# Turning the centred rows of the first and last batch on TensorE, with later weight loads and paired score tiles

## The chip, the core and the metric

The kernel runs on one core of one Trainium2 chip, as one launch. The metric is the device time of that launch in microseconds (us), the median of several executions. A profile of one execution says what each engine did: PE is TensorE's matmuls and PEld its weight loads, DVE is VectorE, ACT ScalarE, POOL GpSimd, and SP the queue from which most transfers are issued.

## The reference

Two layers follow each other. The first is a block-sparse causal attention over 4 batches, 8 heads, 768 positions of 64 numbers: each query sees its own block of 64 keys and the three blocks (of 12) whose mean key scores highest.

```python
k_rep = k.reshape(B, H, n_blocks, block, D).mean(axis=3)
gate_scores = np.einsum('bhsd,bhnd->bhsn', q, k_rep)       # causal blocks only
top_idx = np.argsort(gate_scores, axis=-1)[..., -top_k:]   # plus the query's own block
scores = np.where(mask & causal, scale * q @ k.T, -1e9)
out = softmax(scores) @ v
```

The second takes the heads side by side as rows x of 512 numbers, mixes them by a Fourier transform over positions and columns, and puts them through two matrices:

```python
u = x + np.real(np.fft.fft(np.fft.fft(x, axis=1), axis=2))
un = (u - mean(u)) / np.sqrt(var(u) + 1e-06)
out = u + np.maximum(un @ w_ch1, 0.0) @ w_ch2      # w_ch1 512 x 2048, w_ch2 2048 x 512
```

## The kernel before, in words

**Pairs and slots.** Two heads make a pair; 4 pairs make a batch, 16 pairs in all. `attn_slot(i, g, a)` holds the attention work of one slot: the six score tiles of pair i (`stage_S(i, 0..5)`), the gate of pair i+1 (`stage_G`), the turning of q and k of pair i+2 (`stage_A`: twelve 128x128 transposes on TensorE into two PSUM tiles, a reduction `kr` and a copy `q32` on DVE, a cast of the keys on ACT, a copy of the queries on POOL), and the product with v of pair i-1 (`stage_V`, one half for each head, after which DVE divides into the rows x and `stage_fold` adds and subtracts them for the Fourier step). The loads of later pairs are issued on SP at the places where the slot frees their buffers: v of pair i+1 after `cast_v(i-1)`, k and q of pair a+3 after `stage_A(a)`.

**Two kinds of scores.** For the first seven pairs (`P < NX`, NX = 7) a score matmul contracts over 64 rows, the two heads standing in the two halves of the array, and more 64-row matmuls add the mask. From pair 7 on the mask stands in 32 further rows (96 rows, one head at a time), and the gate is `stage_G2` with `stage_K`.

**A batch's second layer.** `stream(b)` is a list of steps: `stage_fg` (DVE), `stage_Y` twice and `stage_M` three times (Fourier steps on TensorE; M's result is added to x on DVE as u, and ACT writes the centred rows, u minus its mean, over x in f16), the turning of these rows into `unT` (six transposing DMAs on SP, in `stage_M`), `stage_R` (variance on DVE, inverse root on POOL), sixteen `stage_W1` (unT with w1, then a relu on ACT or DVE) and `stage_W2` for six row tiles, the last four of which (`held`) are kept for the next batch's stream. In the stream of batch b, `hold_loads` stops the issuing of input loads from before `stage_fg` until `free_loads` after `stage_M`, so that the transposing DMAs meet an empty SP queue; before batch 0 it is called already ahead of slot 4.

**What sets the order.** Slots 1 to 4 run alone; then, for each batch, `weave` merges four slots with one stream: each step has a weight, and the list goes on with whichever of the two has used the smaller share of its own total. A step of weight w that does nothing holds the other steps of its list back by that share. The prologue's order is the written order on every engine. After it the written order binds the SP queue alone; on the other engines a planner, which takes the written order as priority and estimates when operands and buffers are free, sets an order at build time, and each engine then runs its own list strictly in order. All PSUM tiles come from one pool of 4 buffers of two banks each, so a matmul that starts a new tile may have to wait for the engine that reads an old one.

**The constants and weights.** `consts_first` loads the identity and pair 0 and builds `indz` (two 128x768 tiles for the mask) on POOL. The tables `FS` and `FD` for the Fourier steps are loaded on SP ahead of slot 1's loads. w1 comes in four POOL loads (1 MB read each, cast to f16), each behind a one-element POOL copy (`gate`) that reads the weights `pt` of a pair and so sets the earliest time: in the order `load_w1(0,0)`, slot 1, `load_w1(1,1)`, slot 2, `load_w1(2,2)`, slot 3, `load_w1(3,3)`, slot 4.

Of the kernel before, what the change touches and what calls it, by code (L numbers as in the profile page):

```python
# [11 lines left out]
FP = mybir.dt.float32  # L12
# [7 lines left out]
S = 768  # L20
DM = 512
NB = 12
# [106 lines left out]
def kernel(  # L129
# [33 lines left out]
    def ctile(shape, dtype, name):  # L163
        return cpool.tile(shape, dtype, tag=f"c_{name}", name=name)
# [8 lines left out]
    fs_sb = ctile([128, 2, 2, 3, KE], F16, "fs_sb")  # L173
    fd_sb = ctile([128, 6, 256], F16, "fd_sb")
    id32 = ctile([128, 128], FP, "id32")
    oth = ctile([128, 10, NB], F16, "oth")
    czl = ctile([128, 32], F16, "czl")
    czr = ctile([128, S - Q0], F16, "czr")
# [273 lines left out]
    def stage_M(b, kp):  # L452
        u_b, x_b = bpool.tile([128, 2, DM], FP, tag="u_b", name=f"u{kp}_{b}", bufs=5), x_t[b]
        u_t[b, kp] = u_b
        mps = pst([128, 2, 512], f"mx{kp}_{b}")
        for k2 in range(2):
            kt = 2 * kp + k2
            sg = 0 if kt < 3 else 1
            rows = slice(128 * (kt % 3), 128 * (kt % 3 + 1))
            for par in range(2):  # L460
                src = ys[b, par][sg]
                o = mps[:, k2, 256 * par:256 * par + 256]
                nc.tensor.matmul(o, src[:, 0, rows], fd_sb[:, 3 * par, :], start=True, stop=False)
                nc.tensor.matmul(o, src[:, 1, rows], fd_sb[:, 3 * par + 1 + sg, :], start=False,
                                 stop=True)
        if kp == 0:
            un_t[b] = bpool.tile([128, NDT, S], F16, tag="unT", name=f"unT_{b}", bufs=1)
            st_t[b] = [bpool.tile([128, *sh], FP, tag=n, name=f"{n}_{b}", bufs=2)
                       for n, sh in (("mv", [NST, 2]), ("rs", [NST]), ("sm", [NST]))]
        sm = st_t[b][2]  # L470
        for k2 in range(2):
            kt = 2 * kp + k2
            nc.vector.scalar_tensor_tensor(  # L473
                out=u_b[:, k2, :].rearrange("p (m two) -> p two m", two=2),
                in0=mps[:, k2, :].rearrange("p (two m) -> p two m", two=2), scalar=1.0,
                in1=x_b[:, kt, :].rearrange("p (m two) -> p two m", two=2),
                op0=ALU.mult, op1=ALU.add, accum_out=sm[:, kt:kt + 1])
        nm = spool.tile([128, 2], FP, tag="nm", name=f"nm{kp}_{b}")
        nc.vector.tensor_scalar(out=nm, in0=sm[:, 2 * kp:2 * kp + 2],  # L479
                                scalar1=-0.0625 / DM, scalar2=None, op0=ALU.mult)  # L480
        for k2 in range(2):
            nc.scalar.activation(out=x_b[:, 2 * kp + k2, :], in_=u_b[:, k2, :],  # L482
                                 func=AF.Identity, scale=0.0625, bias=nm[:, k2:k2 + 1])
        for kt in range(2 * kp, 2 * kp + 2):
            nc.sync.dma_start_transpose(un_t[b][:, :, 128 * kt:128 * kt + 128], x_b[:, kt, :])

# [60 lines left out]
        nc.gpsimd.tensor_copy(out=dst, in_=src)  # L547

    def consts_first():
        nc.scalar.dma_start(id32, dr["ident32"].ap())  # L550
        load(0, 1, nc.sync)
        load(0, 0, nc.scalar)
        nc.vector.memset(dummy, 1.0)
        nc.scalar.activation(out=dummy, in_=dummy, func=AF.Exp)
        nc.vector.memset(wsrc, 0.0)
        wps = pst([128, 512], "warmps")
        for _ in range(16):
            nc.tensor.matmul(wps, wsrc[:, 0:128], wsrc, start=True, stop=True)  # L558
        nc.vector.tensor_copy(out=dummy, in_=wps[:, 0:1])
        nc.gpsimd.memset(czl, 0.0)  # L560
        nc.gpsimd.memset(czr, 0.0)
        nc.vector.memset(lt, 0.0)
        nc.gpsimd.memset(czl2, 0.0)
        nc.gpsimd.memset(czr2, 0.0)
        for i in range(NSLOT):
            nc.gpsimd.memset(kr_s[i], 0.0)
            nc.gpsimd.memset(kr2_s[i], 0.0)
        for i in range(NVS):
            nc.gpsimd.memset(v_s[i][:, :, :, 64:66], 1.0)
        nc.scalar.dma_start(half, dr["half"].ap().rearrange("p (e n) -> p e n", e=2))  # L570
        nc.scalar.dma_start(czl[0:NB, :], dr["czl"].ap())
        nc.scalar.dma_start(czr[0:NB, :], dr["czr"].ap())
        nc.scalar.dma_start(indc, dr["indc"].ap())
        load(1, 1, nc.sync)
        load(1, 0, nc.sync)
        nc.scalar.dma_start(oth, dr["oth"].ap().rearrange("p (b n) -> p b n", n=NB))
        for w in range(2):
            pcopy(indz[w].rearrange("p (n c) -> p n c", c=64),
                  indc[:, NB * w:NB * w + NB].rearrange("p (x o) -> p x o", o=1)
                  .to_broadcast([128, NB, 64]), [NB, 64])  # L580

    def consts_next():
        nc.sync.dma_start(oth2, dr["oth2"].ap())
# [26 lines left out]
    def attn_slot(i, g, a):  # L610
        L = []

        def add(P, w, f):
            if P is not None and 0 <= P < NPAIR:
                L.append((f, w))

        def sa():
            stage_A(a)
            load(a + 3, 1, nc.sync)
            load(a + 3, 0, nc.sync)  # L620

        def v1():
            stage_V(i - 1, 1)
            stage_fold(*divmod(i - 1, NP))

        add(i - 1, 0.0, lambda: cast_v(i - 1))
        add(i, 0.45, lambda: stage_S(i, 0))
        add(g, 0.4, lambda: stage_G(g))
        add(i, 0.45, lambda: stage_S(i, 1))
        add(a, 1.3, sa)  # L630
        add(i, 0.45, lambda: stage_S(i, 2))
        add(i - 1, 0.6, lambda: stage_V(i - 1, 0))
        if g is not None and g >= NX:
            add(g, 0.0, lambda: stage_K(g))
        add(i, 0.45, lambda: stage_S(i, 3))
        add(i - 1, 0.6, v1)
        add(i, 0.45, lambda: stage_S(i, 4))
        add(i, 0.12, lambda: stage_S(i, 5))
        return L

    def w2(b, sts):
# [1 line left out]

    def stream(b):
        held = w2(b - 1, [2, 3]) + w2(b - 1, [4, 5]) if b else []
        L = [(hold_loads, 0.0), (lambda: stage_fg(b), 0.0)] + held[0:1]
        L += [(lambda h=h: stage_Y(b, h), 0.5) for h in range(2)]
        L += [(lambda kp=kp: stage_M(b, kp), 0.3) for kp in range(3)]
        L += [(free_loads, 0.0), (lambda: stage_R(b), 10.0 if b == 0 else 3.0)]
        L += held[1:]  # L650
        if b == 0:
            L += [(lambda c=c: load_w2(c, 5 + c // 2), 0.0) for c in range(4)]
        W1 = [(lambda it=it: stage_W1(b, it), 1.3) for it in range(NIT)]
# [52 lines left out]
        stage_S(0, 5)  # L706
    with tc.manual_schedule(engines={ET.SP}):
        kq(5)
        nc.sync.dma_start(fs_sb, dr["FS"].ap())
        nc.sync.dma_start(fd_sb, dr["FD"].ap())  # L710
        load_w1(0, 0)
        run(attn_slot(1, 2, 3))
        load_w1(1, 1)
        run(attn_slot(2, 3, 4))
        load_w1(2, 2)
        run(attn_slot(3, 4, 5))
        load_w1(3, 3)
        consts_next()
        hold_loads()
        run(attn_slot(4, 5, 6))  # L720
        for b in range(B):
            L = []
# [33 lines left out]
```

## Time and profile before

| | |
|---|---|
| median of 3 runs | 333.23 us (331.92 to 334.62) |
| the profiled execution's own time | 331.54 us |
| its span, first to last instruction | 329.8 us |
| PE busy | 299.6 us (91%) |
| DVE, ACT, POOL busy | 191.4, 165.3, 114.9 us |
| mean granted TensorE clock | 0.974 |

The page's forty slices of 8.2 us show the engine's busy share, the granted clock of TensorE and the use of the DMA engines, in tenths:

```profile
PE   8599784876999999989999999999999999799994
DVE  1778858599472929896364629984414379121211
PEclk9989979697999999999999999999999999999999
DMA  9999999747999244049900004055000103500022
```

A 9 is 90% or more; PEclk is the clock granted, 9 being close to the upper of its two levels (2.4 GHz) for the whole slice.

### The profile page before, as it was taken

The numbers are of one execution on the slowest core, as the hardware profiler recorded it, in microseconds if no ns is written. First come the engines' busy times: TensorE is split into PE (matmuls) and PEld (weight loads), VectorE is DVE, ScalarE is ACT, GpSimd is POOL, SyncE is SP. The second block draws the span as 40 slices with busy tenths as digits, with TensorE's granted clock in tenths as the row PEclk, the third lists the DMA queues.
The fourth block names the chain that finished last, engine by engine and source line by source line (L and its number), as shares of the span: only waits on it lengthen the run. The fifth ranks groups of instructions, "written<-read, shape, count | busy, mean of one in ns | idle before, by whom it ended". The sixth has DMA issues, their size and how long they took to land.

```text
span 329.8 us, 6632 instructions
## 1 busy us (share of the span) xinstructions
PE 299.6 (91%) x2594; PEld 178.9 (54%) x2594; DVE 191.4 (58%) x570; ACT 165.3 (50%) x203; POOL 114.9 (35%) x257
## 2 busy tenths in 40 slices
PE   8599784876999999989999999999999999799994
PEld 4356563553666655645666656655665564355441
DVE  1778858599472929896364629984414379121211
ACT  1377855277667544574776634537573124234000
POOL 2467374304936744436381513334220000200000
PEclk9989979697999999999999999999999999999999
DMA  9999999747999244049900004055000103500022
GB/s 175 217 228 218 253 211 201 127 76 149 194 216 223 49 81 111 3 95 250 211 5 0 2 1 113 18 100 157 0 2 0 47 19 75 151 0 2 0 97 95
DMA packets 95371, 34.40 MB, mean 104 GB/s; under 512 B 89120, under 2 KB 91500, under 8 KB 95340
## 3 DMA queue, kind: packets, MB, share of 16 engines
q1 hardware_dynamic: 90460, 29.26, 41.0%
q0 software_dynamic: 2688, 4.19, 7.5%
q10 hardware_dynamic: 2192, 0.52, 0.9%
q8 instruction: 20, 0.33, 0.4%
q14 instruction: 11, 0.09, 0.1%
HBM read 28.73 MB, written 6.29 MB: 106 GB/s over the span
## 4 chain that ended last, share of the span: by engine, by line
PE 67%; DVE 17%; ACT 7%; DMA 4%; issue 2%; SPq 1%; POOL 1%; DVEq 0%
PE c L533 19%; PE h L515 17%; PE h L517 9%; PE sc L353 5%; PE av L379 4%; PE tp L244 3%; DMA nat<-in_v_dram 3%; ACT x L482 2%; PE yp L432 2%; ACT pt L363 2%; DVE u L473 2%; PE warmps L558 2%; DVE zw L167 2%; DVE kr L247 2%; PE sc L348 2%
## 5 line engine op out<-in xcount | busy, mean ns | idle before, releaser
L363 ACT ACTIVATE pt<-sc 128x1024 f16<-128x1024 f32 x96 | 84.7, 916 | 56.5 <-PE sc L353 42.0
L533 PE MATMUL c<-w_sb,hT 128*128 128x512 f16 x384 | 86.9, 379 | 0.3 <-ACT pt L363 0.3
L515 PE MATMUL h<-unT,w_sb 128*128 128x512 f16 x256 | 85.8, 380 | 0.6 <-ACT pt L363 0.6
L517 PE MATMUL h<-unT,w_sb 128*128 128x256 f16 x256 | 69.7, 272 | 2.4 <-DMA unT<-x 2.4
L366 POOL TENSOR_SCALAR_AFFINE_SELECT pt<-pt 128x256 f16<-128x256 f16 x96 | 41.5, 443 | 79.0 <-ACT pt L363 78.6
L533 PEld LDWEIGHTS <-hT 128*128 128x128 f16 x384 | 36.9, 98 | 41.6 <-issue 0.9
L524 ACT ACTIVATE hT<-h 128x768 f16<-128x768 f32 x48 | 38.8, 812 | 31.5 <-PE h L517 31.3
L522 DVE TENSOR_SCALAR hT<-h 128x768 f16<-128x768 f32 x16 | 15.3, 956 | 42.9 <-PE h L517 42.8
L515 PEld LDWEIGHTS <-w_sb 128*128 128x128 f16 x256 | 24.9, 97 | 28.0 <-issue 1.3
L539 DVE SCALAR_TENSOR_TENSOR u<-c,rs,u 128x512 f32<-128x512 f32 x24 | 17.1, 740 | 39.1 <-PE c L533 39.1
L353 PE MATMUL sc<-qk 96*128 96x512 f16 (+3 forms) x144 | 28.2, 306 | 1.8 <-ACT pt L363 1.4
L379 PE MATMUL av<-v,pt 128*128 128x65 f16 x672 | 26.6, 195 | 3.6 <-POOL v L170 2.1
L379 PEld LDWEIGHTS <-pt 128*128 128x128 f16 x672 | 24.4, 98 | 9.6 <-issue 5.5
L517 PEld LDWEIGHTS <-w_sb 128*128 128x128 f16 x256 | 25.0, 98 | 7.7 <-DMA unT<-x 2.9
L170 POOL TENSOR_SCALAR_AFFINE_SELECT qk<-q 64x768 f16<-64x768 f32 (+1 forms) x25 | 20.6, 825 | 16.3 <-DVE q L262 15.1
L244 PE MATMUL tp<-id,nat 128*128 128x128 f32 x192 | 24.5, 276 | 0.7 <-DVE tr L447 0.3
L170 POOL TENSOR_SCALAR_AFFINE_SELECT v<-nat 128x768 f16<-128x768 f32 x16 | 15.1, 944 | 26.0 <-DMA nat<-in_v_dram 25.9
L244 PEld LDWEIGHTS tp<-id,nat 128*128 128x128 f32 x192 | 21.2, 141 | 3.8 <-issue 1.5
L348 PE MATMUL sc<-qk 64*128 64x512 f16 (+3 forms) x112 | 16.4, 335 | 6.3 <-ACT qk L250 2.9
L170 POOL TENSOR_SCALAR_AFFINE_SELECT qk<-mt 32x384 f16<-32x384 f16 x36 | 18.4, 512 | 8.3 <-DVE mt L290 6.4
L482 ACT ACTIVATE x<-u,nm 128x512 f16<-128x512 f32 x24 | 15.7, 712 | 9.5 <-DVE nm L479 9.5
L257 ACT CAST qk<-tp 64x768 f16<-64x768 f32 x18 | 14.3, 794 | 9.6 <-DVE kr L247 9.5
(82 smaller groups left out, 340.6 us busy)
## 6 DMA issues: line engine op xcount, KB each, us to landing
nat<-in_k_dram SPq DMA_DIRECT2D x32, 192.0 KB, 5.6
nat<-in_v_dram SPq DMA_DIRECT2D x16, 384.0 KB, 5.0
nat<-in_q_dram SPq DMA_DIRECT2D x30, 192.0 KB, 4.5
out_dram<-u SPq DMA_DIRECT2D x11, 512.0 KB, 3.4
w_sb<-in_moe_w_ch_dram POOLq DMA_DIRECT2D x8, 512.0 KB, 7.3
fs_sb<-c_FS SPq DMA_DIRECT2D x1, 582.0 KB, 7.7
out_dram<-u SPq DMA_DIRECT2D x2, 256.0 KB
nat<-in_q_dram ACTq DMA_DIRECT2D x2, 192.0 KB, 5.2
```

Of the source, the lines that this page charges most:

```text
L170: nc.gpsimd.affine_select(out=out, in_=in_, pattern=[[0, i] for i in n], base=0, channel_multiplier=0, compare_op=ALU.is_ge, fill=0.0)
L244: nc.tensor.transpose(ps[:, 128 * st:128 * st + 128], src[:, st, :], id32)
L348: nc.tensor.matmul(ps[:, e, co:co + q1 - q0], qk[hs[e], 1, XW(P), 128 * jt:128 * jt + 128], qk[hs[e], 0, XW(P), q0:q1], start=(co == 0), s ...
L353: nc.tensor.matmul(ps[:, e, co:co + q1 - q0], qk[0:96, e, 1, 128 * jt:128 * jt + 128], qk[0:96, e, 0, q0:q1], start=True, stop=True)
L363: nc.scalar.activation(out=pt[:, o:o + 2 * n].rearrange("p (e c) -> p e c", e=2), in_=ps[:, :, 0:n], func=AF.Exp, scale=0.125)
L366: nc.gpsimd.affine_select(out=dg, in_=dg, pattern=[[0, 2], [1, 128]], base=0, channel_multiplier=-1, compare_op=ALU.is_ge, fill=0.0)
L379: nc.tensor.matmul(av[:, e, 66 * st:66 * st + 65], pt[:, co:co + 128], vv[:, e, jt, 0:65], start=(cnt == 0), stop=(cnt == 20))
L482: nc.scalar.activation(out=x_b[:, 2 * kp + k2, :], in_=u_b[:, k2, :], func=AF.Identity, scale=0.0625, bias=nm[:, k2:k2 + 1])
L515: nc.tensor.matmul(hp[:, 0:512], w1s, unT[:, dt, 0:512], start=(dt == 0), stop=(dt == NDT - 1))
L517: nc.tensor.matmul(hp[:, 512:768], w1s, unT[:, dt, 512:768], start=(dt == 0), stop=(dt == NDT - 1))
L524: nc.scalar.activation(out=hT, in_=hp, func=AF.Relu)
L533: nc.tensor.matmul(cps[:, part, :], h_t[b, it][:, 128 * st:128 * (st + 1)], w2_sb[:, it, :], start=(it == 0), stop=(it == NIT - 1))
```

## The change

The centred rows of batches 0 and 3 are turned by TensorE (24 f16 transposes of 128x128 in three steps `stage_T`, each into a PSUM tile that DVE, and for the last step DVE and ACT, copy into `unT`); batches 1 and 2 keep the transposing DMAs. The stream of batch 0 gets empty steps of weight 5, 4, 2 and 2 and `stage_R` after the turning with weight 2 instead of 10; loads are held in batches 1 and 2 alone. In the last batch the T steps stand between the held W2 steps. The slots 1 to 6 write the score tiles in twos. FS and FD are loaded after slot 2, the four w1 loads after slots 1, 2, 3 and 3. The first k and q are loaded one head on SP and one on ACT, and `indz` is built on ACT.

```diff
+    id16 = ctile([128, 128], F16, "id16")
...
+        if b not in (0, B - 1):
+            stage_T(b, kp)
+
+    def stage_T(b, kp):
+        x_b = x_t[b]
+        if b in (0, B - 1):
+            ps = pst([128, NDT, 256], f"xt{kp}_{b}", F16)
+            for k2 in range(2):
+                for dt in range(NDT):
+                    nc.tensor.transpose(ps[:, dt, 128 * k2:128 * k2 + 128],
+                                        x_b[:, 2 * kp + k2, 128 * dt:128 * dt + 128], id16)
+            dst = un_t[b][:, :, 256 * kp:256 * kp + 256]
+            if kp < 2:
+                nc.vector.tensor_copy(out=dst, in_=ps)
+            else:
+                nc.vector.tensor_copy(out=dst[:, :, 0:128], in_=ps[:, :, 0:128])
+                nc.scalar.copy(out=dst[:, :, 128:256], in_=ps[:, :, 128:256])
+            return
         for kt in range(2 * kp, 2 * kp + 2):
             nc.sync.dma_start_transpose(un_t[b][:, :, 128 * kt:128 * kt + 128], x_b[:, kt, :])
...
-        nc.scalar.dma_start(id32, dr["ident32"].ap())
-        load(0, 1, nc.sync)
-        load(0, 0, nc.scalar)
+        for who in (1, 0):
+            src = (q, k)[who]
+            t = apool.tile([128, NST, 2, 64], FP, tag=f"nat{who}", name=f"nat{who}_0", bufs=3)
+            nat[0, who] = t
+            for e, eng in ((0, nc.sync), (1, nc.scalar)):
+                eng.dma_start(t[:, :, e, :], src[0, e].rearrange("(st p) d -> p st d", p=128))
+                if who == 1 and e == 0:
+                    nc.scalar.dma_start(id32, dr["ident32"].ap())
...
+        nc.vector.tensor_copy(out=id16, in_=id32)
...
-            pcopy(indz[w].rearrange("p (n c) -> p n c", c=64),
+            nc.scalar.copy(out=indz[w].rearrange("p (n c) -> p n c", c=64),
...
-        add(i, 0.45, lambda: stage_S(i, 0))
-        add(g, 0.4, lambda: stage_G(g))
...
+        if i < NX:
+            order = [S[0], S[1], G, (sa, 1.3), S[2], S[3], V[0], K, V[1], S[4], S[5]]
+        else:
+            order = [S[0], G, S[1], (sa, 1.3), S[2], V[0], K, S[3], V[1], S[4], S[5]]
...
-        L = [(hold_loads, 0.0), (lambda: stage_fg(b), 0.0)] + held[0:1]
+        L = [(hold_loads if 0 < b < B - 1 else (lambda: None), 0.0), (lambda: stage_fg(b), 0.0)] + held[0:1]
+        if b == 0:
+            L += [(lambda: None, 5.0)]
         L += [(lambda h=h: stage_Y(b, h), 0.5) for h in range(2)]
         L += [(lambda kp=kp: stage_M(b, kp), 0.3) for kp in range(3)]
-        L += [(free_loads, 0.0), (lambda: stage_R(b), 10.0 if b == 0 else 3.0)]
-        L += held[1:]
+        T = [(lambda kp=kp: stage_T(b, kp), 0.6) for kp in range(3)]
+        R = [(free_loads, 0.0), (lambda: stage_R(b), 2.0 if b == 0 else 3.0)]
+        if b == 0:
+            L += [(lambda: None, 4.0), T[0], (lambda: None, 2.0), T[1], (lambda: None, 2.0), T[2]]
+            L += R
+        elif b == B - 1:
+            L += held[1:2] + T[0:1] + held[2:3] + T[1:3] + R + held[3:]
+        else:
+            L += R + held[1:]
...
-        nc.sync.dma_start(fs_sb, dr["FS"].ap())
-        nc.sync.dma_start(fd_sb, dr["FD"].ap())
-        load_w1(0, 0)
         run(attn_slot(1, 2, 3))
-        load_w1(1, 1)
+        load_w1(0, 1)
         run(attn_slot(2, 3, 4))
-        load_w1(2, 2)
+        nc.sync.dma_start(fs_sb, dr["FS"].ap())
+        nc.sync.dma_start(fd_sb, dr["FD"].ap())
+        load_w1(1, 2)
         run(attn_slot(3, 4, 5))
+        load_w1(2, 3)
         load_w1(3, 3)
         consts_next()
-        hold_loads()
         run(attn_slot(4, 5, 6))
```

## Rows read from the trace of the kernel before

**Rows 1.** Busy time by stretch: stretch, length, then PE, PEld, DVE, ACT, POOL busy, clock, DMA.

```profile
28.66:35.82 7.16, 6.50 (x110) 4.53 (x104) 6.27 (x22) 5.88 (x7) 4.96 (x10) 1.00 1.11 258
35.82:45.87 10.05, 7.61 (x111) 5.21 (x106) 6.19 (x22) 5.99 (x7) 5.21 (x11) 0.86 1.02 228
45.87:54.28 8.41, 6.79 (x110) 4.65 (x105) 7.49 (x24) 5.80 (x7) 3.93 (x7) 0.96 1.09 208
53.80:80.30 26.50, 18.35 (x194) 11.72 (x192) 22.57 (x67) 15.37 (x20) 10.03 (x18) 0.81 0.60 116
80.30:265.60 185.30, 181.21 (x1560) 109.34 (x1558) 110.56 (x332) 103.72 (x127) 75.69 (x162) 1.00 0.41 87
265.60:284.00 18.40, 15.92 (x101) 8.95 (x102) 14.41 (x40) 5.95 (x8) 2.40 (x12) 1.00 0.31 56
```

**Rows 2.** Timeline, slot 3: start, duration, engine, line, operation, count, idle before and releaser.

```profile
28.14 2.77 SPq L709 DMA_DIRECT2D fs_sb<-c_FS  x1
...
32.79 0.38 SPq L214 DMA_DIRECT2D nat<-in_v_dram  x1
...
41.20 0.91 POOL L170 TENSOR_SCALAR_AFFINE_SELECT v<-nat 128x768 f16<-128x768 f32 x1 [3.34 <-DMA nat<-in_v_dram]
...
42.16 0.80 PE L379 MATMUL av<-v,pt 128*128 128x65 f16 x21 [2.07 <-POOL v L170]
```

**Rows 3.** Timeline, one turn of slot 2: gate, key reduction, key cast, score tile.

```profile
29.56 0.74 PE L309 MATMUL g<-q,kr 128*32 128x320 f32 x8 [0.37 <-DVE x L167]
...
31.09 0.82 DVE L319 MAX8 mx<-gt 128x8 f32<-128x12 f32 x10
...
32.14 0.95 DVE L247 TENSOR_REDUCE kr<-tp 128x12 f32<-128x768 f32 x1
...
33.13 0.80 ACT L250 CAST qk<-tp 128x768 f16<-128x768 f32 x1 [1.10 <-DVE kr L247]
...
33.98 0.40 PE L348 MATMUL sc<-qk 64*128 64x384 f16 x4 [0.29 <-ACT qk L250]
```

**Rows 4.** Timeline, slots 4 to 6 and the first Fourier steps.

```profile
52.44 0.39 PE L348 MATMUL sc<-qk 64*128 64x384 f16 x4 [1.54 <-ACT qk L250]
...
58.59 1.31 PE L432 MATMUL yp<-fs_sb,fg 128*128 128x193 f16 x7 [3.78 <-DVE fg L415]
...
63.19 1.03 DVE L447 CAST tr<-yp 128x768 f16<-128x768 f32 x1 [3.00 <-ACT ty L445]
...
80.33 0.53 PE L515 MATMUL h<-unT,w_sb 128*128 128x512 f16 x1
```

**Rows 5.** Timeline, the last batch: held W2 work, transposing DMAs, first W1 tile.

```profile
272.26 9.01 PE L533 MATMUL c<-w_sb,hT 128*128 128x512 f16 x41
...
276.05 5.21 SPq L485 DMA_TRANSPOSE unT<-x  x4
...
283.85 0.28 PE L517 MATMUL h<-unT,w_sb 128*128 128x256 f16 x1 [2.37 <-DMA unT<-x]
```

**Rows 6.** Timeline, the prologue: building `indz`, and the first mask matmuls.

```profile
10.12 1.76 POOL L170 TENSOR_SCALAR_AFFINE_SELECT indz<-indc 128x768 f16<-128x768 f16 x2 [7.62 <-DMA indc<-c_indc]
...
13.66 0.32 PE L359 MATMUL sc<-mt,indz 64*128 64x256 f16 x4 [0.54 <-DVE mt L324]
```

**Rows 7.** The page's DMA queues: packets, MB, share of 16 engines' span (POOL's loads).

```profile
q0 software_dynamic: 2688, 4.19, 7.5%
```

**Rows 8.** Timeline, weight loads at a change between 64-row and other matmuls.

```profile
30.37 0.11 PEld L348 LDWEIGHTS <-qk 64*128 64x128 f16 x4 [0.40 <-issue]
...
30.89 1.29 PEld L244 LDWEIGHTS tp<-id,nat 128*128 128x128 f32 x12 [0.18 <-issue]
...
30.89 1.53 PE L244 MATMUL tp<-id,nat 128*128 128x128 f32 x12
```

**Rows 9.** The page's costliest groups: the f32 transposes; count, busy, mean ns, idle before.

```profile
L244 PE MATMUL tp<-id,nat 128*128 128x128 f32 x192 | 24.5, 276 | 0.7 <-DVE tr L447 0.3
```

**Rows 10.** Busy time by stretch of `stage_R`'s statistics alone (line 492): DVE, clock, DMA.

```profile
53.80:80.30 26.50, 3.98 (x6) 0.81 0.60 116
```

More of the change, by code (lines that the diff above doesn't have):

```diff
@@ L577, in consts_first @@
         for w in range(2):
-            pcopy(indz[w].rearrange("p (n c) -> p n c", c=64),
-                  indc[:, NB * w:NB * w + NB].rearrange("p (x o) -> p x o", o=1)
-                  .to_broadcast([128, NB, 64]), [NB, 64])
+            nc.scalar.copy(out=indz[w].rearrange("p (n c) -> p n c", c=64),
+                           in_=indc[:, NB * w:NB * w + NB].rearrange("p (x o) -> p x o", o=1)
+                           .to_broadcast([128, NB, 64]))
     def consts_next():
@@ L626, in attn_slot @@
         add(i - 1, 0.0, lambda: cast_v(i - 1))
-        add(i, 0.45, lambda: stage_S(i, 0))
-        add(g, 0.4, lambda: stage_G(g))
[L629 to L638, printed above, removed]
+        S = [(lambda x=x: stage_S(i, x), 0.45 if x < 5 else 0.12) for x in range(6)]
+        G = (lambda: stage_G(g), 0.4)
+        K = (lambda: stage_K(g) if g >= NX else None, 0.0)
+        V = [(lambda: stage_V(i - 1, 0), 0.6), (v1, 0.6)]
+        if i < NX:
+            order = [S[0], S[1], G, (sa, 1.3), S[2], S[3], V[0], K, V[1], S[4], S[5]]
+        else:
+            order = [S[0], G, S[1], (sa, 1.3), S[2], V[0], K, S[3], V[1], S[4], S[5]]
+        for f, w in order:
+            P = g if (f, w) in (G, K) else a if f is sa else i - 1 if (f, w) in V else i
+            add(P, w, f)
         return L
@@ L708 @@
         kq(5)
+        run(attn_slot(1, 2, 3))
+        load_w1(0, 1)
+        run(attn_slot(2, 3, 4))
         nc.sync.dma_start(fs_sb, dr["FS"].ap())
         nc.sync.dma_start(fd_sb, dr["FD"].ap())
-        load_w1(0, 0)
-        run(attn_slot(1, 2, 3))
-        load_w1(1, 1)
-        run(attn_slot(2, 3, 4))
-        load_w1(2, 2)
+        load_w1(1, 2)
         run(attn_slot(3, 4, 5))
+        load_w1(2, 3)
         load_w1(3, 3)
         consts_next()
-        hold_loads()
         run(attn_slot(4, 5, 6))
```

## The prediction, made before the changed kernel was built or run

> **What bounds the kernel now.** I read the busy time by stretch first, then the chain of waits, and then the timeline at each place where the chain leaves TensorE. By stretch [rows 1], everything from 80.3 to 265.6 us is TensorE's: 181.2 of 185.3 us busy at the full clock. Nothing there can be won but work taken from TensorE itself. The idle time lies ahead of it. The stretch 53.8 to 80.3 has PE busy for 18.35 of 26.5 us at a mean clock of 0.81, while DVE is busy for 22.57: DVE is what limits it. Slot 3 (35.8 to 45.9) took 10.05 us where slot 2 took 7.16, with the clock down to 0.86.
>
> Slot 3 lost its time to a transfer [rows 2]: v of pair 2 was issued at 32.79 and POOL could cast it only at 41.20, after 3.34 us of waiting; TensorE stood for 2.07 us behind that cast and then ran the next few microseconds at the lower clock. The DMA share is above 1.0 in all of slots 2 to 4 [rows 1], so the load was late because the queue ahead of it was long.
>
> An ordinary slot is a ring [rows 3]: the gate matmuls wait for DVE to have read the product with v out of PSUM (0.37), then come the ten maxima (0.82), the key reduction (0.95), the key cast on ACT, which idled 1.10 for it, and a score tile that waited 0.29 for the PSUM buffer which the cast releases. In slot 4 that last wait is 1.54 [rows 4]. Then the first Fourier step waits 3.78 us for `stage_fg`, with attention work of slot 5 queued behind it on PE; DVE itself idles 3.00 us until the Fourier result has come back; the first W1 matmul runs at 80.33. At the end, six transposing DMAs take so long to issue that the held W2 work (41 matmuls, 9.01 us) is over before they land, and PE idles 2.37 [rows 5].
>
> **The change part by part.** The sum is made against the profiled execution, 331.54 us (span 329.8), which lies 1.69 below the median of the runs.
>
> *Start: 0.* Building `indz` leaves POOL, where it took 1.76 us from 10.12 [rows 6], for ACT. A cast of 768 columns takes ACT 0.80 [rows 3], so two end at about 11.7 and the first key cast, now behind them, at 12.5. The mask matmuls that end the first score tile wait for DVE until 13.66 [rows 6]; that is the cover, 1.1 us of it. If ACT needed twice as long, 0.5 would show. The split of the first loads keeps two transfers on each queue ahead of everything else, and `id16` adds one small DVE copy: together between a gain and a loss of 0.3, taken as nothing.
>
> *Later loads: -2.9.* FS and FD stood on SP between 28.14 and 32.79 right ahead of v [rows 2]: 4.65 us. Each of the eight POOL loads took 7.5% of 329.8 us over 8, or 3.1 us of all 16 engines [rows 7]; three w1 loads were ahead of that v's landing and one of them moves behind it. So v lands by about 41.2 - 4.65 - 3.1 = 33.4, and POOL was free for it at 37.9. The wait goes, and slot 3 should look like slot 2: 10.05 - 7.16 = 2.9. The floor is the bare idle, 2.07; the ceiling adds the 0.4 by which POOL's cast also ran late. Late next are the tables, behind slot 2's loads instead of ahead of slot 1's: they land near 50, the first Fourier step needs FS at about 56. w1 is wanted only at W1, some 20 us after its last load is issued.
>
> *Scores in twos: -0.5.* Going from 64-row matmuls to others costs 0.18 of weight-load idle, and coming from the gate 0.40 [rows 8]. A slot loses three such changes; at 0.18 that is 0.54, or 2.2 over slots 1 to 4. But PE has slack there (6.50 busy of 7.16), and the ring above does not run over these changes. It runs over the key cast, and now both halves of the product with v stand behind two score tiles for PSUM. Upwards the price is one half, 0.80 [rows 2], for each of four slots: 3.2. Between -2.2 and +3.2 I take a little gain, since DVE, with 6.27 of 7.16 busy [rows 1], leaves at most 0.9 in a slot, and slot 4 has the 1.54 wait to give.
>
> *First batch: -1.7.* The empty step of weight 5 lets slot 5's scores, gate and transposes run before the Fourier steps, so PE's 3.78 and DVE's 3.00 of idle are filled. That pays only as far as DVE allows. DVE's work up to W1 was 22.57. Take off the statistics, which now follow the turning: 3.98 [rows 10]. Add the copies of the turned rows: a PSUM copy of 768 columns took 1.03 [rows 4], so 1024 take 1.37, twice, and a half of 0.69: 3.4. Add what slot 6 now does earlier, by the weights: its gate and the transposes of pair 8, 0.82 + 0.95 + 0.95 and about 1.3 of small steps [rows 3], 4.0. That makes 26.0 in a stretch of 26.5. With 1.3 of DVE idle in place of 3.93 it lasts 27.3, 0.8 longer, but at its end PE has done one more set of transposes (1.53 [rows 8]) and two score tiles (0.5 each): 2.5. Net 1.7. With DVE never idle it is 3.0; with as much idle as before it is a loss of 0.9; copies at no cost, inside that idle, would give 5. The turning on PE costs nothing here, as PE has over 8 us idle. The statistics then run under W1, where DVE is busy for 110 of 185 us [rows 1]. Unheld input loads fill a DMA that was used to 0.60.
>
> *Last batch: -0.4.* The 2.37 of idle [rows 5] goes, and 24 transposes come onto PE's path. The lower price is an f16 matmul by columns: 9.01 us over 41 of 512 columns [rows 5] is 0.22, so 0.055 for 128, 1.3 in all. The upper is the f32 transpose, 1.53 over 12 or 0.13 [rows 8], 3.1 in all. I take the middle, 0.08 or 1.9, since the operation is that of the one and the type that of the other. So between -1.1 and +0.7, taken at -0.4. DVE's copies (3.4) go ahead of the statistics there; the inverse root is needed only after the sixteen W1 tiles.
>
> Sum: -2.9 - 0.5 - 1.7 - 0.4 = -5.5, so 326.0 for an execution like the profiled one and, with the 1.69, **327.7** as the median.
>
> **The rivals.**
>
> *DVE takes the gain back.* The late v is repaired, but DVE's added copies and its order keep the stretch before W1 as long as its PE gain: -2.9 + 0.9 and nothing else, 331.2 as a median. For it: DVE has 22.57 of 26.5 already. Against: 3.00 of its idle has one cause [rows 4], which the empty step removes. That the planner undoes the written pairs or the empty steps, so that this part of the change does not happen, ends at the same time. Chance 0.24.
>
> *PSUM in the paired slots (slower).* The place is the first half of the product with v. It now asks for a PSUM buffer after two score tiles, and the buffers are with those tiles, whose exponentials stand behind the key cast on ACT, and with the two turned tiles. If ACT casts first, both halves (0.80 each) follow the cast, where now a score tile and one half do; with an exponential (about 0.9, ACT's 5.9 a slot over six and a cast) before the buffer is free, a slot gets 0.8 + 0.9 - 0.5, 1.2 longer. Over slots 1 to 6 that is 7.2, and 327.7 + 0.5 + 7.2 = 335.4. It decides from the point at which the cast ends over 0.8 after the second score tile. For it: the cast is already what a score tile waits for [rows 3]; against: exponentials that are ready earlier can go first. Chance 0.09.
>
> *Transposes run singly.* A transpose lasted 276 ns on average [rows 9], though twelve were through in 1.53 [rows 8]. Were they not to overlap in the last batch, 24 x 0.276 = 6.6 in place of 1.9 would stand there: 327.7 + 4.7 = 332.4. In the first batch PE's idle covers it. Chance 0.04. [...]
>
> *More than forecast.* DVE never idles before W1 (3.0 in place of 1.7), the saved changes all show (2.2) and f16 transposes go at the matmul rate (1.1): -2.9 - 2.2 - 3.0 - 1.1 = -9.2, 324.0; with cheap copies 322. Chance 0.17.
>
> **How the numbers follow.** The forecast itself, a gain of 3.3 to 7.5, has 0.46. About 1% (3.3 us) is what a measurement of this kernel can tell from no change. Faster by more than that takes the forecast and the case above it: 0.63. Within 1% are the DVE and the transposes rival: 0.28. Slower is the PSUM rival: 0.09. The range goes from 321, below the cheap copies, to 333, which takes in the DVE and the transposes rival and leaves out PSUM.
>
> **What would show it.** In the profile after: no wait of POOL's cast for v in slot 3, and slot 3 near 7.2; slots 1, 2 and 4 no longer than 7.2, 7.2 and 8.4 (else PSUM); no idle of 3 us before the first Fourier step; DVE over 90% busy from there to the first W1 matmul, which should come near 78 with one more `stage_A` done; its copies at 1.0 to 1.4 each; transposes 0.055 to 0.13 apart; no PE idle before the last batch's W1, and the clock at 1.00 there. The prediction is wrong if the first W1 matmul comes after 80, or if FS lands after 56 and the Fourier step waits for the table instead.

## The result, and the profile after

The changed kernel takes 323.95 us (median of four executions, 322.33 to 324.66) against 332.58 for the kernel before on the same chip: a ratio of 0.972 (95% interval 0.966 to 0.978). Run again on another chip it took 325.19 against 332.59: 0.978 (0.974 to 0.982). Executions over 1.5% longer than the fastest of their kernel are left out of all ratios and intervals, and the differences between two variants below are between the means of the others. The forecast was 327.7 in a range of 321 to 333. The gain is 8.6 us by the medians and 9.2 by the ratio on the first chip, 7.4 and 7.3 on the second: above the forecast's 5.5, and on the first chip as much as the 9.2 of the case "more than forecast", which was priced at 324.0.

The profiled execution took 322.33 us, 9.2 less than the one of before, with a span of 320.6 us and a mean clock of 0.995. The page's slices (8.0 us each) show where: the clock is full from the fourth slice on, where before it sagged in the sixth, eighth and tenth, and the dip of PE near the end is gone.

```profile
PE   7598879777999999989999999999999999999995
DVE  1668899996626458974545549984314379421211
PEclk9989999999999999999999999999999999999999
DMA  9999999899990431179600022144000101100023
```

The stretches that answer those of [rows 1], in the same columns: slots 2, 3 and 4, slot 5's first score tile to the free run of W1, the long middle, and the last batch up to its W1.

```profile
27.99:35.34 7.35, 6.18 (x111) 4.32 (x109) 5.84 (x22) 5.77 (x7) 4.97 (x11) 1.00 0.95 195
35.34:42.68 7.34, 6.17 (x110) 4.31 (x108) 5.80 (x22) 5.77 (x7) 4.52 (x11) 1.00 1.13 222
42.68:50.02 7.34, 6.17 (x110) 4.31 (x108) 7.17 (x24) 5.87 (x7) 5.40 (x10) 1.00 1.14 237
50.02:75.83 25.81, 19.43 (x255) 13.59 (x252) 25.14 (x84) 18.83 (x25) 9.30 (x18) 1.00 1.03 212
75.80:258.24 182.44, 177.98 (x1520) 107.07 (x1521) 106.10 (x317) 100.14 (x123) 73.55 (x162) 1.00 0.36 78
258.24:275.07 16.83, 16.73 (x122) 10.15 (x123) 14.70 (x41) 6.60 (x9) 0.17 (x1) 1.00 0.09 33
```

Slot 3 fell from 10.05 to 7.34 us and slot 4 from 8.41 to 7.34. DVE is busy for 25.14 of 25.81 us before W1, so it is what limits that stretch in this profile. The last batch's 16.83 us have PE busy for 16.73. To cut the 9.2 us into parts I use places that both traces have: the first score tile of slot 1 and of slot 5, the first Fourier matmul of batches 1 and 3, and the end.

| us | before | after | change |
|---|---|---|---|
| up to slot 1 | 21.81 | 21.12 | -0.7 |
| slots 1 to 4 | 32.47 | 28.90 | -3.6 |
| slot 5 to the Fourier step of batch 1 | 76.98 | 73.89 | -3.1 |
| from there to the Fourier step of batch 3 | 134.35 | 134.33 | 0.0 |
| from there to the end | 64.19 | 62.36 | -1.8 |

The timeline of slots 3 and 4 (columns as in [rows 2]) shows v of pair 2 cast at 34.98, where it was 41.20, after 0.39 us of waiting. It also shows what the paired tiles cost: the product with v, now in one piece of 42 matmuls, waits 0.80 us for an exponential on ACT.

```profile
34.98 0.91 POOL L170 TENSOR_SCALAR_AFFINE_SELECT v<-nat 128x768 f16<-128x768 f32 x1 [0.39 <-DMA nat<-in_v_dram]
35.35 2.54 SPq L215 DMA_DIRECT2D nat<-in_v_dram  x1
...
38.68 0.55 POOL L624 DMA_DIRECT2D w_sb<-in_moe_w_ch_dram  x1 [0.18 <-POOL w_sb L566]
...
40.80 1.44 PE L380 MATMUL av<-v,pt 128*128 128x65 f16 x42 [0.80 <-ACT pt L364]
42.11 0.89 POOL L170 TENSOR_SCALAR_AFFINE_SELECT v<-nat 128x768 f16<-128x768 f32 x1 [1.97 <-DMA nat<-in_v_dram]
...
47.10 0.70 SPq L745 DMA_DIRECT2D fs_sb<-c_FS  x1
```

In the first batch (timeline, same columns) the Fourier step starts without a wait, where it waited 3.78 in [rows 4]. But the statistics (L511) begin at 64.59, ahead of the first copy of turned rows at 66.05: they did not go behind the turning. W1 starts at 73.77 and runs freely from 75.83, when the last third of the rows is there.

```profile
53.64 0.76 PE L433 MATMUL yp<-fs_sb,fg 128*128 128x193 f16 x7
...
55.38 0.91 POOL L170 TENSOR_SCALAR_AFFINE_SELECT v<-nat 128x768 f16<-128x768 f32 x1 [5.37 <-DMA nat<-in_v_dram]
...
64.59 0.69 DVE L511 BATCH_NORM_STATS2 bst<-u 128x6 f32<-128x512 f32 x1
64.60 0.90 PE L494 MATMUL xt<-id,x 128*128 128x128 f16 x8
...
66.05 0.68 DVE L498 COPY unT<-xt 128x1024 f16<-128x1024 f16 x1
...
69.64 1.53 PE L245 MATMUL tp<-id,nat 128*128 128x128 f32 x12
...
73.77 0.39 PE L534 MATMUL h<-unT,w_sb 128*128 128x512 f16 x1
...
74.44 1.25 DVE L511 BATCH_NORM_STATS2 bst<-u 128x6 f32<-128x512 f32 x2
...
75.83 0.27 PE L536 MATMUL h<-unT,w_sb 128*128 128x256 f16 x1
```

The view of the tile of turned rows gives the new operations' prices: min/median/max in ns, first and last start in us.

```profile
L494 PE MATMUL xt<-id,x x48: 216/219/230, 64.6 to 271.6; 128*128 128x128 f16 x48
L498 DVE COPY unT<-xt x4: 672/680/692, 66.0 to 271.7; 128x1024 f16<-128x1024 f16 x4
L500 DVE COPY unT<-xt x2: 412/414/416, 73.8 to 272.2; 128x512 f16<-128x512 f16 x2
L501 ACT COPY unT<-xt x2: 585/586/586, 74.7 to 272.7; 128x512 f16<-128x512 f16 x2
```

At the end (timeline of the last batch) sixteen transposes stand between the held W2 matmuls, and W1 follows without idle, where 2.37 us were lost in [rows 5].

```profile
270.73 1.06 PE L494 MATMUL xt<-id,x 128*128 128x128 f16 x16
...
271.62 3.62 PE L552 MATMUL c<-w_sb,hT 128*128 128x512 f16 x16
...
275.07 0.38 PE L534 MATMUL h<-unT,w_sb 128*128 128x512 f16 x1
```

### The profile page after: what moved, and what is told of

It is laid out like the page before. It is cut to its first block, busy times and chain, and to the rows that moved or that the text cites. A ratio compares the mean times of both kernels' runs of the same rounds, so it can differ in the third digit from the quotient of the medians.

```text
span 320.6 us, 6711 instructions
## 1 busy us (share of the span) xinstructions
PE 296.0 (92%) x2642; PEld 178.3 (56%) x2642; DVE 190.2 (59%) x577; ACT 167.5 (52%) x207; POOL 110.8 (35%) x255
## 4 chain that ended last, share of the span: by engine, by line
PE 69%; DVE 17%; ACT 5%; POOL 4%; DMA 2%; issue 2%; SPq 0%; DVEq 0%; POOLq 0%
PE c L552 22%; PE h L534 16%; PE h L536 8%; PE sc L354 6%; PE av L380 4%; PE tp L245 4%; ACT pt L364 2%; DVE x L167 2%; DMA nat<-in_v_dram 2%; PE warmps L582 2%; DVE u L558 2%; DVE u L474 2%; DVE tr L448 1%; DVE zw L167 1%; DVE q L263 1%
## 5 line engine op out<-in xcount | busy, mean ns | idle before, releaser
L367 POOL TENSOR_SCALAR_AFFINE_SELECT pt<-pt 128x256 f16<-128x256 f16 x96 | 40.1, 429 | 74.6 <-ACT pt L364 74.1
L380 PE MATMUL av<-v,pt 128*128 128x65 f16 x672 | 25.5, 193 | 4.6 <-ACT pt L364 2.4
L349 PE MATMUL sc<-qk 64*128 64x512 f16 (+3 forms) x112 | 15.0, 316 | 5.2 <-DVE x L167 2.0
```

The lines of the kernel that those rows point to most:

```text
L367: nc.gpsimd.affine_select(out=dg, in_=dg, pattern=[[0, 2], [1, 128]], base=0, channel_multiplier=-1, compare_op=ALU.is_ge, fill=0.0)
L380: nc.tensor.matmul(av[:, e, 66 * st:66 * st + 65], pt[:, co:co + 128], vv[:, e, jt, 0:65], start=(cnt == 0), stop=(cnt == 20))
```

## The experiments

Ratios are to the kernel before on the same chip, with 95% intervals. Their half-width is about 0.5%, or 1.6 us, so differences between two variants of under 2 us are read from the traces, and only where these show a cause. Single profiles vary as well: the stretch from W1 to the next Fourier step, with nearly the same work in all, took from 47.85 to 52.85 us.

**1. The later loads alone** (the kernel before with the new order of FS, FD and w1).

```diff
-        nc.sync.dma_start(fs_sb, dr["FS"].ap())
-        nc.sync.dma_start(fd_sb, dr["FD"].ap())
-        load_w1(0, 0)
         run(attn_slot(1, 2, 3))
-        load_w1(1, 1)
+        load_w1(0, 1)
         run(attn_slot(2, 3, 4))
-        load_w1(2, 2)
+        nc.sync.dma_start(fs_sb, dr["FS"].ap())
+        nc.sync.dma_start(fd_sb, dr["FD"].ap())
+        load_w1(1, 2)
         run(attn_slot(3, 4, 5))
+        load_w1(2, 3)
```

> The kernel before with the later table and w1 loads alone. Theory (the steps add up, as in the sum): the wait of POOL's cast for v in slot 3 goes, slot 3 takes about 7.2 us in place of 10.05, and the time is 2.7 to 3.0 us below the kernel before. Rival (the slots merely arrive earlier at a first batch that is limited by DVE and by the held loads, so the gain is taken back there): slot 3 is short, but the first W1 matmul still runs near 80 and the time is within 1 us of the kernel before.

Measured 328.95 us, 0.989 (0.984 to 0.994). Slot 3 became 7.54 us, as expected, but slots 1 to 4 together won only 1.0 us, because the late transfer moved on by one slot. Its timeline:

```profile
38.13 1.41 SPq L214 DMA_DIRECT2D nat<-in_v_dram  x1
...
38.76 0.55 POOL L599 DMA_DIRECT2D w_sb<-in_moe_w_ch_dram  x1 [0.18 <-POOL w_sb L547]
...
48.42 0.91 POOL L170 TENSOR_SCALAR_AFFINE_SELECT v<-nat 128x768 f16<-128x768 f32 x1 [6.36 <-DMA nat<-in_v_dram]
...
49.38 0.49 PE L379 MATMUL av<-v,pt 128*128 128x65 f16 x11 [2.68 <-POOL v L170]
```

v of pair 3 was issued at 38.13 with two w1 loads right behind it and landed ten us later. In the profile of the whole change it was issued at 35.35, earlier ahead of them, and landed in time; experiment 5 shows an execution of the same kernel in which it did not. The profiled execution won 2.2 us, 0.9 of it before slot 1, and the ratio says 3.6; in how many executions v is late can't be seen.

**2. Without pairs** (the changed kernel with the old order of score tiles).

```diff
-        if i < NX:
+        if False:
```

> The changed kernel with the score tiles of slots 1 to 6 in the old order. Theory (the ring of PSUM buffers and the key cast sets the slot, not the changes of matmul shape): slots 2 and 3 go back from 7.35 to about 7.16, slot 4 from 7.34 to about 8.4, so 0.5 to 1 us slower than the changed kernel, and not more. Rival (each change of shape costs its 0.18): 2.2 us slower over slots 1 to 4, with slots 2 and 3 at 7.7 or more. Second rival (pairs only cost): 0.5 us faster.

Measured 325.88, 0.981 (0.975 to 0.986). The slots took 6.86, 7.15, 7.10 and 8.04 us, against 6.87, 7.35, 7.34 and 7.34 with pairs. So the twos cost 0.2 in an ordinary slot and win 0.7 in slot 4, where the wait of a score tile for the key cast is 1.18 again: 0.25 in all. Slot 5 to the next Fourier step took 76.83 instead of 73.89, at a clock of 0.94 instead of 1.00 up to W1. Variants with the pairs took 75.0 to 77.7 there (experiments 3, 8, 9, 10 and 11), so I don't put this on the pairs. The median does not settle what the pairs are worth: the ratio is 0.003 above experiment 5's, 0.9 us, and so within the noise.

**3. The last batch by DMA** (the changed kernel with `if b == 0` in place of `if b in (0, B - 1)`, and the old list for the last stream).

> The changed kernel with the last batch turned by the transposing DMAs again and its steps in the old order; the first batch stays on TensorE. Theory (24 transposes take 1.3 to 1.5 us of TensorE and remove 2.4 us of idle): 0.9 to 1.2 us slower than the changed kernel, with PE idle 2.4 us ahead of the second W1 matmul of the last batch. Rival (the whole 1.85 us by which the stretch from the last Fourier step to the end became shorter belongs to the turning): 1.8 us slower.

Measured 325.84, 0.980 (0.975 to 0.985). From the last Fourier step to the end it took 62.42 us, no longer than with TensorE. Its idle ahead of W1 was short:

```profile
275.42 1.77 SPq L561 DMA_DIRECT2D out_dram<-u  x2
276.61 0.28 PE L536 MATMUL h<-unT,w_sb 128*128 128x256 f16 x1 [1.05 <-DMA unT<-x]
```

The six transposing DMAs took 7.75 us to issue here as in experiment 1, where the same wait was 2.69. So the idle that TensorE's turning removes is 1.0 to 2.7 us, by execution. Where it is 1.05, the turning buys nothing in the trace: from the first Fourier step of the batch to the second W1 matmul it took 16.93 us here and 17.05 with TensorE. The ratio is 0.002 above experiment 5's, 0.6 us, within the noise.

**4. The first batch by DMA** (the changed kernel with `if b == B - 1` in place of `if b in (0, B - 1)`: batch 0 is turned by DMA at its T steps, with input loads not held).

> The changed kernel with the first batch's rows turned by transposing DMAs issued at the places of its three turning steps, loads not held. Theory (what TensorE's turning buys in the first batch is independence of a loaded SP queue): the DMAs stand behind input loads on SP, the first W1 matmul comes 3 us or more later than 75.8, and the time is 1.5 to 4 us above the changed kernel. Rival (the turning itself buys nothing, since DVE limits this stretch and is spared 1.8 us of copies): within 0.5 us of the changed kernel or faster.

Measured 341.64, 1.028 (1.020 to 1.035): slower than before, and by its ratio 16 us above the changed kernel, where 1.5 to 4 were expected. The transposing DMAs stand in the SP queue between loads of q, k and v, and W1 waits for them:

```profile
76.00 2.61 SPq L504 DMA_TRANSPOSE unT<-x  x2
...
79.33 4.22 SPq L504 DMA_TRANSPOSE unT<-x  x2
...
90.60 2.79 SPq L504 DMA_TRANSPOSE unT<-x  x2
90.70 0.59 PE L534 MATMUL h<-unT,w_sb 128*128 128x512 f16 x1 [17.06 <-DMA unT<-x]
```

So with input loads not held, turning by DMA is no choice here, while TensorE's turning does not stand in that queue. What TensorE's turning is worth in the first batch against DMAs with the loads held, all else as changed, was not run and stays open.

**5. The changed kernel again**, on another chip.

> The changed kernel once more, unaltered, as the yardstick for the experiments beside it. From the first W1 tile of batch 0 to the first Fourier step of batch 1 it took 48.1 us in one profile, and the same instructions took 49.2 in a variant that differs only in the last batch. Theory (that stretch varies by executions, with the landing of transfers): it lies between 48 and 50 again and the median within 1.5 us of 324.0. Rival (the variant's last batch somehow reaches back): 48.1 again.

Measured 325.19, 0.978 (0.974 to 0.982). Its profiled execution took 330.75 us with a granted clock of 0.95 from start to end, so its lengths are not compared. But it shows the wait of experiment 1 in the unaltered kernel: v of pair 3 was issued at 37.33 with the two w1 loads behind it at 38.08 and 38.99, POOL waited 7.87 us for it, and slot 4 took 9.72 us where slots 1 to 3 took 6.93, 7.41 and 7.40.

```profile
37.33 0.66 SPq L215 DMA_DIRECT2D nat<-in_v_dram  x1
...
47.41 0.89 POOL L170 TENSOR_SCALAR_AFFINE_SELECT v<-nat 128x768 f16<-128x768 f32 x1 [7.87 <-DMA nat<-in_v_dram]
```

In experiment 7 it was issued at 36.83, only half a us earlier, and cast at 42.97; slot 4 took 7.60 there.

**6. The Fourier steps early** (the changed kernel without the empty step of weight 5; the later one has 9 instead of 4, so that the total stays).

```diff
         if b == 0:
-            L += [(lambda: None, 5.0)]
...
-            L += [(lambda: None, 4.0), T[0], (lambda: None, 2.0), T[1], (lambda: None, 2.0), T[2]]
+            L += [(lambda: None, 9.0), T[0], (lambda: None, 2.0), T[1], (lambda: None, 2.0), T[2]]
```

> The changed kernel without the empty step of weight 5 ahead of the first batch's Fourier steps, the 5 added to the empty step behind them, so that W1 keeps its place. Theory (the empty step fills the wait for stage_fg and DVE's idle with attention work of slot 5): PE waits 3 us or more before the first Fourier matmul again, DVE idles about 3 us after it, and the time is 1.5 to 3 us above the changed kernel. Rival (only the order of W1 counts, and the waits are made up before W1): within 0.5 us.

Measured 328.17, 0.988 (0.983 to 0.993): 3.4 us more than experiment 5 on the same chip. The wait of [rows 4] is back:

```profile
54.10 1.31 PE L433 MATMUL yp<-fs_sb,fg 128*128 128x193 f16 x7 [3.16 <-DVE fg L416]
```

Busy time by stretch, as in [rows 1], shows a clock of 0.66 and DVE busy for only 6.39 of 10 us with it:

```profile
50.00:60.00 10.00, 6.84 (x52) 4.46 (x54) 6.39 (x15) 3.87 (x6) 4.88 (x10) 0.66 1.00 228
60.00:70.00 10.00, 7.90 (x112) 5.74 (x110) 9.37 (x36) 7.88 (x12) 2.73 (x4) 1.00 1.17 205
```

**7. The wide copies twice** (the two 1024-column copies of batch 0 done twice: 1.36 us more on DVE, nothing else).

```diff
             if kp < 2:
-                nc.vector.tensor_copy(out=dst, in_=ps)
+                for _ in range(2 if b == 0 else 1):
+                    nc.vector.tensor_copy(out=dst, in_=ps)
```

> The changed kernel with each of the two wide DVE copies of turned rows in batch 0 done twice: 2 x 0.68 = 1.36 us more on DVE and nothing else. Theory (DVE limits the stretch up to the first W1 tile, so the copies that came out at 0.68 and not at the forecast's 1.37 are where the forecast was short): the first W1 tile comes 1.0 to 1.4 us later and the time is 1 to 1.4 above the changed kernel. Rival (DVE has slack there, the copies are hidden): within 0.3 us, and the extra gain lies elsewhere.

Measured 326.05, 0.980 (0.976 to 0.984), 0.6 more than experiment 5, which is within the noise and lies between the theory and the rival. From slot 5 to the free run of W1 it took 28.46 us instead of 25.81, with DVE busy for 27.60:

```profile
50.26:78.72 28.46, 21.73 (x270) 15.51 (x266) 27.60 (x91) 19.21 (x25) 10.47 (x22) 0.94 1.00 202
```

The 2.65 us between the two profiles can't be put on the copies: with single copies the same stretch took 25.74 us in experiment 3, 27.20 in experiment 10 and 28.39 in experiment 8. So this experiment decides neither way.

**8. The old loads in the changed kernel** (the edit of experiment 1 backwards).

> The changed kernel with the tables and w1 loaded as early as in the kernel before. Theory (the late v of slot 3 is worth what the forecast gave it, once the pairs and the first batch are as changed): POOL's cast for v waits over 3 us in slot 3, slots 1 to 4 take 2.5 to 3.5 us more, and the time is 2.5 to 3.5 above the changed kernel. Rival (the later tables and w1 move the wait to slot 4 or behind it, so the order of loads is worth about 1 us, as in the run of the loads alone): 0.5 to 1.5 us above.

Measured 327.37, 0.986 (0.982 to 0.991). v of pair 2 is late again (POOL waits 4.42 us, PE 2.83), and slots 1 to 4 take 32.01 us, 3.1 more than in the profile of the changed kernel; by the means it is 2.7 us above experiment 5.

**9. Batch 0's copies on ACT.** Experiment 7 asks for the opposite edit: all three copies of batch 0's rows on ACT.

```diff
-            if kp < 2:
+            if b == 0:
+                nc.scalar.copy(out=dst, in_=ps)
+            elif kp < 2:
                 nc.vector.tensor_copy(out=dst, in_=ps)
```

> The changed kernel with all three copies of batch 0's turned rows on ACT: DVE loses 0.68 + 0.68 + 0.41 = 1.77 us in the stretch before the first W1 matmul, ACT gains about 2 us (its half copy took 0.585, so a whole one about 1.0). Theory 1, DVE sets the length of that stretch: with the doubled copies 1.36 us of DVE cost 2.65 us in the trace and 0.9 in the median, so 1.77 less give back 1.1 to 3.4 us; slot 5's first score tile to the first W1 matmul 22.4 to 24.7 us instead of 25.8, ratio to before 0.965 to 0.974. Theory 2, ACT, busy for 18.8 of the 25.8 us, comes to bind, because a wide copy stands ahead of an exponential: 25.8 to 27.5 us, ratio 0.976 to 0.984.

Measured 325.22, 0.975 (0.971 to 0.979): no gain. The stretch took 26.1 us. Busy time by stretch: DVE is full from 60 to 70 us without the copies, with other work in their place, and the clock falls after that.

```profile
60.00:70.00 10.00, 7.24 (x107) 5.39 (x108) 10.00 (x31) 7.69 (x13) 3.50 (x6) 0.99 1.09 183
70.00:80.00 10.00, 9.41 (x113) 6.96 (x111) 5.05 (x26) 8.32 (x11) 4.93 (x11) 0.84 1.07 216
```

In its timeline a score tile now waits for a copy on ACT, as the second theory had it:

```profile
75.45 0.40 PE L349 MATMUL sc<-qk 64*128 64x384 f16 x4 [0.58 <-ACT unT L498]
```

**10. The fourth w1 load behind slot 4**, and **11. both 9 and 10**.

```diff
         load_w1(2, 3)
-        load_w1(3, 3)
         consts_next()
         run(attn_slot(4, 5, 6))
+        load_w1(3, 4)
```

> The changed kernel with the fourth w1 load behind slot 4 instead of slot 3 (behind the weights of pair 4). Theory 1, the fourth load is what makes the v of slot 4 marginal (late by 2.7 us on TensorE with the later loads alone, in time in most traces of the whole change): slots 1 to 4 stay at 28.9 us and are never longer, the median falls by 0 to 0.8, ratio 0.972 to 0.978. Theory 2, the load then collides with the loads of slots 5 and 6 or with w2: the stretch before the first W1 matmul is over 26.5 us instead of 25.8, ratio above 0.98.

> Both of these edits in one kernel. Theory 1, the two act in different stretches (slot 4, and the first batch), so the gains add: ratio 0.963 to 0.974, below either alone. Theory 2, what one wins the other loses in the same transfers: ratio no lower than the better of the two.

Measured 324.87, 0.975 (0.971 to 0.978), and 325.58, 0.980 (0.975 to 0.985). Slots 1 to 4 took 29.10 and 28.90 us, as in the first profile of the changed kernel, where that v was in time anyway; the stretch before W1 took 27.2 and 28.4 us, with a clock of 0.85 and 0.70 from 70 to 80 us. So no gains add up, and none of the three edits is shown to gain anything: 0.975 lies within the interval of the changed kernel's 0.978. What the fourth load behind slot 4 saves in executions like that of experiment 5 is not measured.

**12. The last batch alone** (the kernel before with only the last batch turned by TensorE, T steps between the held W2 steps, and loads not held in that batch; the diff shows the order of the steps).

```diff
-        L += [(free_loads, 0.0), (lambda: stage_R(b), 10.0 if b == 0 else 3.0)]
-        L += held[1:]
+        R = [(free_loads, 0.0), (lambda: stage_R(b), 10.0 if b == 0 else 3.0)]
+        if b == B - 1:
+            T = [(lambda kp=kp: stage_T(b, kp), 0.6) for kp in range(3)]
+            L += held[1:2] + T[0:1] + held[2:3] + T[1:3] + R + held[3:]
+        else:
+            L += R + held[1:]
```

> The kernel before with one part of the change alone: the last batch's rows turned by TensorE, its T steps between the held W2 steps, loads not held there. Theory 1, the 2.37 us of idle ahead of the last batch's W1 go and 24 transposes of 0.056 us come: last Fourier step to the end 62.4 us instead of 64.2, 1.0 us of it in the median: ratio 0.994 to 0.999. Theory 2, the idle of that one execution was an accident of when an output write was issued, and the median sees nothing: ratio 0.999 to 1.003. Either way the slots and the first batch are as before: slot 5's first score tile near 54, the first W1 matmul near 80.

Measured 330.21, 0.991 (0.988 to 0.994): 3.0 us, between 2.0 and 4.0. The tail took 62.5 us in its profile, 1.7 less than before, and the median shows a gain clear of noise. Of the 1.7 only 1.2 lie ahead of W1 (17.05 us from the first Fourier step to the second W1 matmul, against 18.24 before); the other 0.5 come after the last matmul, which the change does not touch. In experiment 3 the DMA was quick in the profiled execution. Why the median gained 3.0 is open: the idle varies (2.69 in experiment 1), and before's one profile need not be typical of it.

## Why the prediction was right, and where its terms were off

**The whole.** The time lies in the forecast's range, and the gain came in the stretches where it was placed. The loads and the pairs came out near their terms; the start, the first batch and the last batch gave more than theirs. Inside the first batch errors of opposite sign cancelled in part, which is luck. Undone one at a time, the loads cost 2.7 us (experiment 8), the empty step 3.4 (6), the pairs 0.9 (2) and the last batch's turning 0.6 (3), each give or take about 1.5, so the last two are within the noise.

**Start, 0: right within 0.3.** Of the 0.7 of the table 0.4 is not the change's: the sixteen warm-up matmuls ahead of everything took between 4.92 and 6.58 us in these profiles, with the same instructions; 5.71 and 5.28 in the two compared. The other 0.3 is open.

**Later loads, -2.9: right for slot 3, wrong on what is late next.** The wait went and slot 3 became 7.34. The prediction named the tables as next, and they made it: FS was issued at 47.10 and the Fourier step had no wait. The next late thing was v of pair 3, behind two w1 loads (experiment 1). In the whole change its margin held in the first profile and failed in the second, where slot 4 took 9.72 us (experiment 5). Where v of pair 3 lands in time, undoing the loads costs 3.1 in these slots (experiment 8); whether it would land in time the forecast did not ask.

**Scores in twos, -0.5: a small gain, as forecast, by two effects of which one was expected.** The traces of experiment 2 give -0.25 in all. Slot 4's 1.54 of [rows 4] went, as named. The ordinary slots got 0.2 longer, and the reason is the mechanism of the PSUM rival: the product with v waits 0.80 for an exponential. Its price was put at 1.2 a slot; it is 0.2, and both halves then run in one piece, 1.44 us for 42 matmuls instead of 0.80 twice [rows 2].

**First batch, -1.7: the size was off, and three entries of DVE's list with it.** The trace gave -3.1; experiment 3, with the same first batch, took 74.95 us where the table has 73.89, which is -2.0, and the kernel before's own first batch took 76.45 and 78.60 in experiments 1 and 12 where the table has 76.98. The list said 26.0 us in 27.3; measured were 25.14 in 25.81. (1) The copies were priced from a 768-column copy of f32, 1.03 us in [rows 4]: 1.37 for 1024 columns and 3.4 in all. They took 0.68 and 1.79. The Trainium skill, "VectorE: DVE Perf Modes", section "Why PSUM operands drop a tier", says that a PSUM operand leaves a copy up to double rate, and single rate for fp32. The trace agrees: 1024 columns of f16 in 0.68 us is twice the rate of 768 columns of f32 in 1.03. (2) The step "take off the statistics, which now follow the turning: 3.98" failed. The planner ran four of the six before the first W1 matmul, from 64.59 on, and the other two at 74.44, before W1 ran freely. (3) The fold and the casts of the Fourier results got cheaper, which no row of before had been read for: `zw` 1.03 us instead of 1.81 (last section), the casts `tr` 1.88 instead of 2.04. Of DVE's idle 0.67 was left, where 1.3 was taken. These three do not close the list: 26.0 + 3.98 - 1.6 is 28.4, and the 3.2 down to 25.14 are more than the third shows. That DVE decides fits the traces, where it is busy for 95 to 99% of this stretch in experiments 3 and 7 to 11, but it is not shown: 1.36 us more of it cost 0.6, within the noise (experiment 7), and 1.77 less gave nothing (experiment 9). The copies' 1.6 us are about the size of the miss, but with the statistics, of opposite sign, in the same list that is no proof. What is shown is the empty step, worth 3.4 us (experiment 6).

**Last batch, -0.4: the row was right, the price was the low end.** Sixteen transposes took 1.06 us and eight 0.61, 0.056 apart, against 0.08 taken. From the first Fourier step of the batch to the second W1 matmul it took 17.05 us instead of 18.24: -1.2, near the -1.1 that the low price gave. The other -0.6 of the tail's -1.8 comes after the last matmul (3.85 us to the end of the span instead of 4.47) and is not the turning's. Experiment 12's median gained more, 3.0, and experiment 3's trace lost nothing, so the size varies by execution.

**The rivals.** DVE did not take the gain back. The transposes did not run singly, and the clock was 1.00 over them. What the "more than forecast" case got right is low prices for transposes and copies. Its profile was also a favourable one: with nearly the same steps the clock from 70 to 80 us was 1.00 there, and 0.84, 0.85 and 0.70 in experiments 9 to 11, where twelve f32 transposes took 2.2 to 2.8 us instead of 1.53. The second chip's ratio of 0.978 is nearer to the forecast's 0.983 than the first chip's 0.972.

**The signs.** Right: no wait of note for v in slot 3 (0.39 us), one more `stage_A` before W1 (69.64), DVE over 90%, no idle ahead of the last W1. Not met: slot 2 at 7.35 instead of 7.2 at most, copies below 1.0, and W1 at 73.77 (freely at 75.83) instead of near 78.

## What to carry to other kernels

Moving a transfer out of the way makes the next one late: look for the next v, not only for the next table, and count what is issued right behind it. Price a PSUM copy by its type as well as its columns. Steps that are written later stay later only where the planner has no slot for them; it filled DVE's time with the statistics, and with other work where ACT took the copies.

## What the runs showed of the hardware

**DVE's f16 additions take longer beside POOL's work.** The same two additions of 768 f16 columns (`zw`) took 1.81 us in the kernel before, with POOL busy all along (timeline):

```profile
55.52 0.94 POOL L170 TENSOR_SCALAR_AFFINE_SELECT v<-nat 128x768 f16<-128x768 f32 x1 [0.81 <-DMA nat<-in_v_dram]
55.73 1.81 DVE L167 TENSOR_TENSOR zw<-sd 128x768 f16<-128x768 f16 x2
56.42 2.06 POOL L366 TENSOR_SCALAR_AFFINE_SELECT pt<-pt 128x256 f16<-128x256 f16 x3
```

and 1.03 us after, with POOL waiting for a late v from 50.0 to 55.38:

```profile
51.59 1.03 DVE L167 TENSOR_TENSOR zw<-sd 128x768 f16<-128x768 f16 x2
```

The Trainium skill, "SBUF — State Buffer", section "SBUF: two separate sides", says that DVE and GpSimd share one pair of ports, which whichever starts first holds for its whole instruction; a DVE instruction with two SBUF inputs competes for it only with a GpSimd one that reads SBUF. These rows agree with that, and so do the other batches and runs: 1.01 to 1.03 us for this pair where POOL was idle or began late in it, 1.20 to 1.81 where POOL worked beside it from early on. No run here varied POOL's work alone, so the cause is argued and not shown. If it is so, a v that is late for POOL, but not for TensorE, even helped.

**A transposing DMA's time depends on what is around it.** Two of them took 2.6 to 4.2 us to issue between loads (experiment 4), and six 7.75 us in a row; the W1 wait behind those varied from 1.05 to 2.69 us behind the same six.
